# Sums and value tiles copied on chip by DMA, their twelve transposes in float32r in one stretch, and the last two quads' transposes inside the first expert slot

## The chip, the cores and the metric

The kernel runs on one core of a Trainium2 chip. The metric is the device time of one execution in microseconds (us), as a median of runs. TensorE (PE, with its weight loads shown apart as PEld), VectorE (DVE), ScalarE (ACT), GpSimd (POOL) and the queue of SyncE (SP), which issues most of the loads, each work their instructions off in order and wait for one another through semaphores. All the PSUM there is, eight banks, is in use during attention.

## The reference

Attention with capped scores over 8 batches, 12 heads, 448 tokens and 64 dimensions; its output, 3584 tokens of 768 values, goes through a gate that picks one of 8 experts for each token, and through that expert's two matrices.

```python
scores = cap * np.tanh(q @ k.T / 8 / cap)
attn = np.exp(scores); attn /= attn.sum(-1) + 1e-9
x = (attn @ v)                       # 3584 x 768 after the heads are joined
logits = x @ w_gate + modality_bias[modality_id]
e = argmax(logits); gate = softmax(logits)[e]
out = gate * (relu(x @ w1[e]) @ w2[e])   # w1 768 x 1024, w2 1024 x 768
```

## The kernel before

The first 351 us are attention, the rest are expert slots (`run_slots`): blocks of up to 384 gathered tokens of one expert, with `ffn1` (x by w1) and `ffn2` (by w2), each value split into two float32r parts.

Attention is worked by **quads**: a quad is four heads of one batch (two pairs, t = 0 and 1), 24 quads (NQ) in all, three to a batch. Scores stand transposed, keys on the partitions. Six steps of a quad are a pair's 128 keys (t, i), and a seventh (`shared`) takes the last 64 keys of both pairs. Each step makes a score tile `sc` (two PSUM banks, pool `ps_s`, two buffers), ScalarE's tanh (`th`) and exp (`pt`, or `sh`), and TensorE's product with the values (`pv`, `pvs`) into `xT`, one PSUM bank per pair, which stays transposed: features by queries.

The order in which the engines get the work is written out by hand. Step i of the main loop has four rounds R0 to R3, and `ORDER` lists for each round what is done and for which quad (an offset to i). `group` is the scores, tanh and exp of the round; R0 has `shared`, each of the others two steps. `pin` keeps the order as written on every engine's queue; what is not pinned (the routing arithmetic of `route`, which the main loop advances by one stage at the end of a round) may be moved by the scheduler.

After its scores, a quad has this to do. `tot1` and `tot2` (DVE) add its probabilities. `xs` (DVE) copies `xT` out of PSUM. `sums` (PE) makes one PSUM tile of gate logits and sums over keys, `gl` (DVE) copies that to SBUF. `lt` (PE) turns it with four float32 transposes into the one-bank PSUM tile `small`; `den` (DVE) reads it there, makes the reciprocals and scales the logits. `tp` (PE) turns each of the two `xs` tiles with four float32 transposes, into the tile `v` (t = 0, shared with `sums`) or `small` (t = 1); `rows` (DVE) scales them and a DMA from POOL writes them to DRAM (`xd`). Before, `lt`, `tp` of t = 0, `den` and `rows` stand in R3 of the next step, `tp` and `rows` of t = 1 in R0 of the one after that.

`fetch` and `fetch_v` load the next quads' tiles through SP. In R3 of the steps in `SPLITS` (12, 14, 15, 17, 18, 20), `split_w` splits a part of the first expert's w1: a cast on ACT behind the round's exps, and a subtraction on DVE that waits for it; both are pinned. At steps 11 and 20, in R0, `early_expert` and `early_full` count tokens with a small matmul `cps` into `small`. After the 24 quads one more step and a round finish the last quads, with the transposes of the first slot's x among them (`MOVES`), and then `ffn1` of the first slot begins; two callbacks run in it, after its blocks f = 1 (the last routing stage) and f = 2 (the plan of all slots, `slots`), which the next gather waits for.

Of the kernel before, what the change touches and what calls it, by code (L numbers as in the profile page):

```python
# [39 lines left out]
F32 = mybir.dt.float32  # L40
# [10 lines left out]
C, CP = 4, 112  # L51
# [28 lines left out]
class Program:  # L80
# [359 lines left out]
    def attention(self, first, rp):  # L440
        tc, nc = self.tc, self.nc
        pe, pin = nc.tensor, self.pin
        with ExitStack() as st:
# [5 lines left out]
            ps_v = st.enter_context(tc.tile_pool(name="ps_v", bufs=1, space=PSUM))  # L449
            quads = [dict(live=i < NQ, kq={}, hl={}, pt={}, tot={}, xT={}, xs={}) for i in range(NQ + 1)]  # L450

# [53 lines left out]
            def group(q, steps):  # L505

                if q >= NQ:
                    return
                ths = []
                made = [scores(q, *step) if step else shared(q) for step in steps]  # L510
                for sc in made:
                    th = pp.tile([128, 2, S], F32, name="th")
                    pin(nc.scalar.activation(th, sc[:, :, :S], AF.Tanh, scale=self.isc))  # L513
                    ths.append(th)
                for step, th in zip(steps, ths):
                    if step:
                        e = quads[q]["pt"][step] = pp.tile([128, 2, S], F32, name="pt", bufs=8)
# [37 lines left out]
            def xs(q, t):  # L555
                x = quads[q]["xs"][t] = self.lp.tile([128, S], F32, name="xT", bufs=4)
                pin(nc.vector.tensor_copy(x, quads[q]["xT"][t][:, :S]))

            def sums(q):
# [11 lines left out]
            def gl(q):  # L571
                quads[q]["gl"] = t = self.lp.tile([128, S], F32, name="gl")
                pin(nc.vector.tensor_copy(t, quads[q]["glog"][:, :S]))

            def lt(q):
                out = self.ps_r.tile([128, 512], F32, name="lt", tag="small")
                for c in range(C):
                    pin(pe.transpose(out[:CP, c * 128 : (c + 1) * 128], quads[q]["gl"][:, c * CP : (c + 1) * CP], self.ident))
                quads[q]["lt"] = out[:CP].rearrange("p (c x) -> p c x", c=C)
# [23 lines left out]
            def tp(q, t):  # L603
                pool, tag = (self.ps_r, "small") if t else (ps_v, "v")
                out = quads[q]["tp"] = pool.tile([128, 512], F32, name="tp", tag=tag)
                for c in range(C):
                    pin(pe.transpose(out[:CP, c * 128 : (c + 1) * 128], quads[q]["xs"][t][:, c * CP : (c + 1) * CP], self.ident))

            def rows(q, t):
                d = quads[q]  # L610
                if t == 0:
                    d["out"] = self.lp.tile([128, C * 256], F32, name="xs", tag="late", bufs=3)[:CP].rearrange("p (c f) -> p c f", c=C)
                pin(nc.vector.tensor_tensor(
                    d["out"][:, :, t * 128 : (t + 1) * 128].rearrange("p c (j d) -> p c j d", j=2),
                    d["tp"][:CP].rearrange("p (c j d) -> p c j d", c=C, j=2),
                    d["rec"][:, :, t].unsqueeze(3).to_broadcast([CP, C, 2, D]),
                    op=ALU.mult,
                ))
                if t:
# [19 lines left out]
            PICK, KNOWN = 3, 6  # L639
            SPLITS = (12, 14, 15, 17, 18, 20)  # L640
            MOVES = {(NQ, 1): (0, 1), (NQ, 2): (2, 3), (NQ, 3): (4, 5)}
            self.warm(self.ps_r, 4)
# [8 lines left out]
            fetch_v(1)  # L651
            for i in range(NQ + 2):
                for r in (1, 0, 2, 3) if i == 0 else range(4 if i <= NQ else 1):
# [4 lines left out]
                    for op, n, *how in ORDER[r]:  # L658
# [13 lines left out]
                    if (i, r) == (1, 1):  # L672
                        self.empty_map()
                    if (i, r) == (PICK * NH + 2, 0):
# [3 lines left out]
                    if (i, r) == (KNOWN * NH + 2, 0):  # L678
# [8 lines left out]
                    if (i, r) == (NQ - 1, 3):  # L687
                        self.make_x()
                    for k in MOVES.get((i, r), ()):
                        self.transpose(k, ps_s, "sc")  # L690
            self.raws = [self.load_raw(e, self.w2, k, DM) for k in range(self.nstage)]
            way = routing[0]
            next(way)
            return early, way

# [12 lines left out]
    def moe_pools2(self, st):  # L708
        pool = lambda name, bufs, **kw: st.enter_context(self.tc.tile_pool(name=name, bufs=bufs, **kw))
        wp = pool("wp2", 1)  # L710
        self.w2s = [[wp.tile([128, DM], F32R, name=f"b{h}{k}") for h in "hl"] for k in range(FC)]
        self.h = [wp.tile([128, FC, W], F32R, name=f"h{h}") for h in "hl"]
        self.ps_h, self.ps_t, self.ps_y = (
            pool("ps_h", 3, space=PSUM), pool("ps_t", 2, space=PSUM), pool("ps_y", 2, space=PSUM)
        )
# [59 lines left out]

    def transpose(self, k, pool, tag, busy=False, n=TW):
        nc = self.nc
        pt = pool.tile([128, 512], F32, name="ptr", tag=tag)
        w = n * 128
        for t in range(n):  # L780
            move = nc.tensor.transpose(
                pt.bitcast(F32R)[:, t * 128 : (t + 1) * 128], self.xg[:, t, k * 128 : (k + 1) * 128], self.identr
            )
            if t == 0:
                self.pin(move)
        hi, lo = self.x[k][:, 0, :w], self.x[k][:, 1, :w]
        if busy:
            self.pin(nc.vector.tensor_copy(hi, pt[:, :w]))
        else:
            nc.scalar.copy(hi, pt[:, :w])  # L790
        nc.vector.tensor_tensor(lo, pt[:, :w], hi, op=ALU.subtract)  # L791

# [60 lines left out]

    def run_slot(self, cur, n, ahead=None, raws=(), between=()):

# [4 lines left out]
        moves, at = [], {}  # L860
        if n == TW:
            self.load_w2(cur[0], raws, range(len(raws) or FC))
        if raws:
            between = (*between, (between[-1][0], lambda: self.load_w2(cur[0], raws, range(len(raws), FC))))
        nxt = ahead() if ahead and not between else None
# [3 lines left out]
        if n < TW:  # L869
            self.load_w2(cur[0], raws)  # L870
        if nxt and nxt[2]:
            self.load_w1(nxt[0])
            moves = [lambda k=k: self.transpose(k, self.ps_t, "ptr", n=nxt[2]) for k in range(KC)]
        elif nxt:
# [7 lines left out]
            }  # L882
        self.ffn2(cur[1], n, between=moves, wait=2 if raws else 0, at=at)
        return nxt
# [89 lines left out]
    def run_slots(self, cur, order):  # L974
# [17 lines left out]
        for i in range(FIXED + 1):  # L992
            if i == FIXED:
                which = nc.values_load(self.plani[0:1, 2:3], min_val=0, max_val=len(ENDS))
            cur = self.run_slot(cur, TW, lambda: ahead(i), *((self.raws, order) if i == 0 else ()))
        self.finish(which, len(ENDS) - 1, cur, ahead)
# [107 lines left out]
    def tail(self, fresh=False):  # L1104
# [4 lines left out]
        with ExitStack() as st:  # L1109
# [4 lines left out]
            with tc.For_i(begin, total, 1) as s:  # L1114
# [9 lines left out]
                for k in range(KC):  # L1124
                    self.transpose(k, self.ps_t, "ptr")
                self.ffn1(TW)
                self.ffn2(mt, TW)

    def build(self):
        tc, nc = self.tc, self.nc  # L1130
        with ExitStack() as st:
# [4 lines left out]
            with ExitStack() as sa:  # L1136
# [6 lines left out]
                with tc.If(big == 0) as branch:  # L1143
                    with ExitStack() as sb:
# [3 lines left out]
                        rt = sb.enter_context(tc.tile_pool(name="rt", bufs=1))  # L1148
                        early, way = self.attention(first, rt)
                        self.moe_pools2(sb)  # L1150
# [78 lines left out]
```

## Time and profile before

| what | us |
|---|---|
| median of 3 runs | 866.61 |
| lowest and highest | 862.97, 867.07 |
| the profiled execution, its own time | 863.48 |
| its span, first to last instruction | 861.9 |

The profile is of one execution. A row of a timeline has the start in us from the span's beginning, the length in us, the engine, the line, and how many equal instructions are merged; a bracket behind it is idle time of the engine just ahead, with what ended it. PE's instructions overlap, so what a piece costs is the distance from its start to the start of the next piece, not its length.

### The profile page before, as it was taken

Reading aid. Unit: us, or ns where it says so; the run is one execution under the profiler, and the core shown is the slowest. Engines: PE = TensorE matmul, PEld = TensorE weight load, DVE = VectorE, ACT = ScalarE, POOL = GpSimd, SP = SyncE. Lnnn points to the kernel's source line nnn. Section 1 sums busy time; section 2 is a strip of 40 time slices with the busy share of each in tenths; the row PEclk is TensorE's granted clock in tenths of the full one; section 3 lists DMA queues with packets and bytes.
Section 4 is the critical chain, followed back from the end, with each engine's and each line's share of the span. In section 5 each row is a group of like instructions: output and inputs, shape, how many; then the busy total and the mean of one; then the engine's idle time right before and its main releaser. Section 6 shows DMA issues by size and latency. Waiting matters only on the chain. (4 is left out here: it accounts for less than half of the span.)

```text
span 861.9 us, 14828 instructions
## 1 busy us (share of the span) xinstructions
PE 843.7 (98%) x5507; PEld 648.3 (75%) x5507; DVE 528.3 (61%) x1017; ACT 529.3 (61%) x685; POOL 136.1 (16%) x157
## 2 busy tenths in 40 slices
PE   8999999999999999999999999999999999999995
PEld 3444444444444444699999999999999999998884
DVE  6789888989898888874443443444334443428640
ACT  6999999999999899534443443444334444325621
POOL 2002020202020222143102020020301102012101
PEclk9999999999999999999999999999999999999999
DMA  7243435273646351456745255473534745237753
GB/s 252 92 146 89 169 90 169 46 261 89 217 89 217 89 182 41 120 186 201 244 140 190 102 160 215 141 253 106 162 146 159 245 141 185 91 129 228 247 196 125
DMA packets 44024, 136.85 MB, mean 159 GB/s; under 512 B 8470, under 2 KB 8862, under 8 KB 43936
## 3 DMA queue, kind: packets, MB, share of 16 engines
q1 hardware_dynamic: 34544, 102.63, 36.7%
q0 software_dynamic: 9248, 33.11, 11.7%
q8 instruction: 47, 0.77, 0.4%
q14 instruction: 41, 0.34, 0.2%
q10 hardware_dynamic: 144, 0.00, 0.0%
HBM read 113.91 MB, written 22.40 MB: 158 GB/s over the span
## 5 line engine op out<-in xcount | busy, mean ns | idle before, releaser
L513 ACT ACTIVATE th<-sc,isc 128x896 f32<-128x896 f32 x168 | 161.2, 1004 | 22.8 <-PE sc L502 15.4
L812 PE MATMUL ph<-x,al 128*128 128x384 f32 (+1 forms) x480 | 156.1, 325 | 0.0
L839 PE MATMUL py<-bh,hh 128*128 128x384 f32 x448 | 153.5, 343 | 1.6 <-ACT hh L818 1.6
L839 PE MATMUL py<-bh,hl 128*128 128x384 f32 x448 | 150.2, 335 | 0.0
L839 PE MATMUL py<-bl,hh 128*128 128x384 f32 x448 | 149.7, 335 | 0.0
L520 ACT ACTIVATE pt<-th,cabs 128x896 f32<-128x896 f32 x144 | 142.1, 1041 | 0.0
L808 PE MATMUL ph<-x,ah 128*128 128x384 f32 x384 | 129.3, 337 | 0.0
L809 PE MATMUL ph<-x,ah 128*128 128x384 f32 x384 | 129.0, 336 | 0.0
L528 PE MATMUL xT<-pt,va 128*64 128x448 f32 x576 | 125.0, 555 | 0.0
L762 DVE TENSOR_TENSOR bl<-raw,bh 128x768 fp32r<-128x768 f32 x80 | 73.5, 954 | 44.6 <-ACT bh L761 41.6
L844 ACT ACTIVATE ot<-py,mt 128x384 f32<-128x384 f32 x56 | 32.6, 582 | 106.6 <-PE py L839 61.9
L761 ACT CAST bh<-raw 128x768 fp32r<-128x768 f32 x80 | 63.5, 839 | 49.5 <-DMA raw<-in_w_dram 45.3
L818 ACT ACTIVATE hh<-ph 128x384 fp32r<-128x384 f32 x64 | 30.6, 490 | 99.4 <-PE ph L812 96.0
L812 PEld LDWEIGHTS ph<-x,al 128*128 128x128 f32 x480 | 90.2, 188 | 0.0
L849 POOL DMA_INDIRECT out_dram<-ot,mt x28 | 31.4, 1122 | 369.1 <-ACT ot L844 339.8
L839 PEld LDWEIGHTS py<-bh,hh 128*128 128x128 f32 x448 | 84.1, 188 | 3.2 <-ACT hh L818 1.9
L819 DVE SCALAR_TENSOR_TENSOR hl<-ph,hh 128x384 fp32r<-128x384 f32 x64 | 34.7, 554 | 83.4 <-ACT hh L818 83.4
L762 DVE TENSOR_TENSOR al<-raw,ah 128x1024 fp32r<-128x1024 f32 x60 | 71.2, 1222 | 22.9 <-ACT ah L761 22.5
L791 DVE TENSOR_TENSOR x<-ptr,x 128x384 fp32r<-128x384 f32 (+1 forms) x60 | 31.2, 540 | 87.8 <-ACT x L790 87.8
L839 PEld LDWEIGHTS py<-bl,hh 128*128 128x128 f32 x448 | 84.2, 188 | 0.0
L839 PEld LDWEIGHTS py<-bh,hl 128*128 128x128 f32 x448 | 84.1, 188 | 0.0
L528 PEld LDWEIGHTS xT<-pt,va 128*64 128x64 f32 x576 | 35.2, 137 | 63.0 <-issue 43.2
(199 smaller groups left out, 1374.1 us busy)
## 6 DMA issues: line engine op xcount, KB each, us to landing
raw<-in_w_dram SPq DMA_DIRECT2D x66, 512.0 KB, 4.8
raw<-in_w_dram SPq DMA_DIRECT2D x86, 384.0 KB, 5.1
kq<-in_kq_dram SPq DMA_DIRECT2D x47, 448.0 KB, 6.5
va<-in_v_dram SPq DMA_DIRECT2D x24, 448.0 KB, 4.9
xd<-xs POOLq DMA_DIRECT2D x24, 448.0 KB, 5.1
mapd<-pay,pos POOLq DMA_INDIRECT x32, 4.0
xg<-xd,mt POOLq DMA_INDIRECT x30, 5.7
first<-in_kq_dram SPq DMA_DIRECT2D x2, 224.0 KB, 3.3
```

The costliest lines, as they stand in the source:

```text
L513: pin(nc.scalar.activation(th, sc[:, :, :S], AF.Tanh, scale=self.isc))
L520: pin(nc.scalar.activation(e, th, AF.Exp, scale=self.cabs))
L528: pin(pe.matmul(xT[j * D : (j + 1) * D, :S], va[:, u * D : (u + 1) * D], quads[q]["pt"][t, i][:, j], start=i == 0, stop=t == 1 and i == KU ...
L761: a = self.nc.scalar.copy(hi, raw)
L762: b = self.nc.vector.tensor_tensor(lo, raw, hi, op=ALU.subtract)
L808: nc.tensor.matmul(ph[:, :w], hi[:, fs], self.x[k][:, 0, :w], start=first, stop=False)
L809: nc.tensor.matmul(ph[:, :w], hi[:, fs], self.x[k][:, 1, :w], start=False, stop=False)
L812: nc.tensor.matmul(ph[:, :w], lo[:, fs], self.x[k][:, 0, :w], start=False, stop=last)
L819: nc.vector.scalar_tensor_tensor(hl[:, f, :w], acc, 0.0, hh[:, f, :w], op0=ALU.max, op1=ALU.subtract)
L839: nc.tensor.matmul(py[:, :HALF], self.h[a][:, f, rows], self.w2s[f][c][:, cs], start=i == 0, stop=i == 3 * FC - 1,)
L844: nc.scalar.mul(ot[:, cs], py[:, :HALF], mt[:, t, 1:2])
L849: self.last_out = nc.gpsimd.indirect_dma_start(self.out, bass.IndirectOffsetOnAxis(ap=mt.bitcast(I32)[:, t, 0:1], axis=0), ot, None, bound ...
```

## The change

`xs` and `gl` each gain an SBUF-to-SBUF DMA on SP's queue (`again`), which makes a float32r copy of the tile, 128 by 448, for all quads but the last. `turn` transposes that copy with the float32r identity. `lt` and both `tp` move to R0 two steps later, in one stretch of twelve transposes, behind `pvs`. `lt` writes into a buffer of the score pool instead of `small` (for the last two quads still `small`). `den` and both `rows` stand behind them in R0; `tot1` stays ahead of `den`, `tot2` goes behind `xs`. `split_hi` and `split_lo` of the next quad go to R2 and R3. R2 has one `pv` step where it had two, R3 three. `pt` has six buffers instead of eight. The counts at steps 11 and 20 go from R0 to R1. `split_w` stays where it was, at the end of R3. After the last quad one shorter list (`LAST`) is left; the transposes of quads 22 and 23 and the last routing stages run inside `ffn1`, after its blocks 0, 1 and 2, the plan after block 3. The first slot's w2 is split after blocks 2 and 3, no longer ahead of `ffn1`.

```diff
+            def again(q, what, src, tag, bufs):
+                if q < NQ - 1:
+                    copy = quads[q]["cp"][what] = self.lp.tile([128, S], F32R, name="cp", tag=tag, bufs=bufs)
+                    self.load(copy.bitcast(F32), src)
+            def turn(q, what, src, out):
+                copy = quads[q]["cp"].get(what)
+                for c in range(C):
+                    cs, to = slice(c * CP, (c + 1) * CP), slice(c * 128, (c + 1) * 128)
+                    if copy is None:
+                        pin(pe.transpose(out[:CP, to], src[:, cs], self.ident))
+                    else:
+                        pin(pe.transpose(out.bitcast(F32R)[:CP, to], copy[:, cs], self.identr))
...
             def lt(q):
-                out = self.ps_r.tile([128, 512], F32, name="lt", tag="small")
+                if q < NQ - 2:
+                    out = ps_s.tile([128, 2, 512], F32, name="sc")[:, 0]
+                else:
+                    out = self.ps_r.tile([128, 512], F32, name="lt", tag="small")
+                turn(q, "gl", quads[q]["gl"], out)
...
             ORDER = (
-                ((group, 0, (None,)), (pvs, -1), (tp, -2, 1), (tot1, -1, 1), (tot2, -1, 1), (rows, -2, 1), (xs, -1, 0)),
-                ((group, 0, ((0, 0), (0, 1))), (pv, -1, 1, 1), (pv, -1, 1, 2), (split_hi, 1, 0), (xs, -1, 1), (split_lo, 1, 0)),
                 (
-                    (group, 0, ((0, 2), (1, 0))), (sums, -1), (pv, 0, 0, 0), (pv, 0, 0, 1),
-                    (split_hi, 1, 1), (split_lo, 1, 1), (gl, -1), (tot1, 0, 0),
+                    (group, 0, (None,)), (pvs, -1), (lt, -2), (tp, -2, 0), (tp, -2, 1), (tot1, -1, 1), (den, -2),
+                    (rows, -2, 0), (rows, -2, 1), (xs, -1, 0), (tot2, -1, 1),
+                ),
+                ((group, 0, ((0, 0), (0, 1))), (pv, -1, 1, 1), (pv, -1, 1, 2), (xs, -1, 1)),
+                (
+                    (group, 0, ((0, 2), (1, 0))), (sums, -1), (pv, 0, 0, 0),
+                    (split_hi, 1, 0), (split_lo, 1, 0), (gl, -1), (tot1, 0, 0),
                 ),
                 (
-                    (group, 0, ((1, 1), (1, 2))), (lt, -1), (tp, -1, 0), (pv, 0, 0, 2), (pv, 0, 1, 0),
-                    (tot2, 0, 0), (den, -1), (rows, -1, 0),
+                    (group, 0, ((1, 1), (1, 2))), (pv, 0, 0, 1), (pv, 0, 0, 2), (pv, 0, 1, 0),
+                    (split_hi, 1, 1), (split_lo, 1, 1), (tot2, 0, 0),
                 ),
             )
+            LAST = (
+                ((pvs, -1), (tot1, -1, 1), (xs, -1, 0), (tot2, -1, 1)),
+                ((pv, -1, 1, 1), (pv, -1, 1, 2), (lt, -2), (xs, -1, 1)),
+                ((sums, -1), (gl, -1)),
+                ((den, -2),),
+            )
...
-                        self.run_slots(early, ((1, lambda: next(way, None)), (2, order)))
+                        w2 = lambda at, *ks: (at, lambda: self.load_w2(early[0], self.raws, range(*ks)))
+                        self.run_slots(early, (*late, w2(2, 0, 4), (3, order), w2(3, 4, FC)))
```

`late` holds three callbacks: after block 0, `tp` of quad 22, `lt` of quad 23, `rows` and `den`; after block 1, `tp` and `rows` of quad 23 and two routing stages; after block 2, the last routing stage.

## Rows read from the trace of the kernel before

**Rows 1.** The page: busy time, share and count of PE, and the granted TensorE clock in 40 slices of the span, in tenths.

```profile
PE 843.7 (98%) x5507; PEld 648.3 (75%) x5507; DVE 528.3 (61%) x1017; ACT 529.3 (61%) x685; POOL 136.1 (16%) x157
PEclk9999999999999999999999999999999999999999
```

**Rows 2.** Busy time by stretch, for a stretch of attention. Columns: length, busy time of each engine, granted clock, DMA share, GB/s.

```profile
50.00:150.00 100.00, 100.00 (x744) 48.06 (x740) 85.09 (x174) 93.19 (x102) 14.47 (x17) 1.00 0.42 130
```

**Rows 3.** Who waited for whom over the whole span: total us, times, longest.

```profile
ACT th L513 <- PE sc L502: 15.4, 23, 3.8
...
SPq L92 <- PE xT L528: 238.8, 20, 14.7
```

**Rows 4.** The timeline of PE over one quad without a cast and without routing, from its first score step (R1) to the next quad's.

```profile
122.93 0.47 PE L502 MATMUL sc<-hi 64*128 64x448 f32 x2
...
124.34 1.72 PE L528 MATMUL xT<-pt,va 128*64 128x448 f32 x8
...
127.41 0.56 PE L569 MATMUL glog<-tot,pick 128*32 128x448 f32 x1
...
129.05 1.72 PE L528 MATMUL xT<-pt,va 128*64 128x448 f32 x8
130.71 0.47 PE L502 MATMUL sc<-hi 64*128 64x448 f32 x2
...
132.11 0.65 PE L578 MATMUL lt<-ident,gl 128*112 128x128 f32 x4
132.60 0.60 PE L607 MATMUL tp<-ident,xT 128*112 128x128 f32 x4
133.13 1.72 PE L528 MATMUL xT<-pt,va 128*64 128x448 f32 x8
134.78 0.98 PE L490 MATMUL sc<-kq 64*64 64x448 f32 x8
...
136.45 0.65 PE L607 MATMUL tp<-ident,xT 128*112 128x128 f32 x4
137.03 0.47 PE L502 MATMUL sc<-hi 64*128 64x448 f32 x2
```

**Rows 5.** The timeline of PE around two runs of six float32r transposes (of x): among full-size matmuls of the first slot, and after the last quad among attention's smaller forms.

```profile
398.55 0.64 PE L781 MATMUL ptr<-identr,xg 128*128 128x128 f32 x6
399.03 0.41 PE L839 MATMUL py<-bh,hh 128*128 128x384 f32 x1
...
354.37 0.70 PE L781 MATMUL ptr<-identr,xg 128*128 128x128 f32 x6
355.00 0.56 PE L569 MATMUL glog<-tot,pick 128*32 128x448 f32 x1
```

**Rows 6.** The timeline of PE at the count of step 11.

```profile
164.86 0.65 PE L607 MATMUL tp<-ident,xT 128*112 128x128 f32 x4
166.29 0.17 PE L290 MATMUL cps<-acc,ones 112*128 112x8 bf16 x1 [0.78 <-DVE xs L613]
```

**Rows 7.** The timeline of ACT: the exp of `shared` in quads 12 and 20, eight quads apart, and in quad 14 the tanh pair of R3, and the cast of `split_w` behind the exps.

```profile
180.42 1.04 ACT L520 ACTIVATE sh<-th,cabs 128x896 f32<-128x896 f32 x1
...
295.57 1.04 ACT L520 ACTIVATE sh<-th,cabs 128x896 f32<-128x896 f32 x1
...
218.21 1.91 ACT L513 ACTIVATE th<-sc,isc 128x896 f32<-128x896 f32 x2 [0.42 <-PE sc L502]
...
221.87 1.04 ACT L761 CAST ah<-raw 128x1024 fp32r<-128x1024 f32 x1
```

**Rows 8.** The same R3 of quad 14: PE's first score step, and the timeline of DVE: the first and the last of `den`'s six instructions, `split_w`'s subtraction, `tot1`.

```profile
217.23 0.47 PE L502 MATMUL sc<-hi 64*128 64x448 f32 x2
...
219.34 0.17 DVE L585 COPY rec<-lt 112x16 f32<-112x16 f32 x1 [0.80 <-PE lt L578]
...
220.11 0.36 DVE L594 TENSOR_TENSOR lg<-lt,rec 112x64 f32<-112x64 f32 x2
...
222.93 1.23 DVE L762 TENSOR_TENSOR al<-raw,ah 128x1024 fp32r<-128x1024 f32 x1 [1.87 <-ACT ah L761]
224.08 1.08 DVE L549 TENSOR_TENSOR tot<-pt 128x896 f32<-128x896 f32 x1
```

**Rows 9.** The timeline of DVE in the quad of rows 4: the copy `gl` behind `sums`.

```profile
129.19 0.62 DVE L573 COPY gl<-glog 128x448 f32<-128x448 f32 x1
```

**Rows 10.** The timeline of PE at the end of attention: the last quad's `pvs`, and the first matmul of `ffn1`.

```profile
351.22 0.98 PE L539 MATMUL xT<-sh,va 64*64 64x448 f32 x8
...
360.67 0.44 PE L808 MATMUL ph<-x,ah 128*128 128x384 f32 x1
```

**Rows 11.** DMA issues: count, KB each, median us from issue to landing.

```profile
kq<-in_kq_dram SPq DMA_DIRECT2D x47, 448.0 KB, 6.5
va<-in_v_dram SPq DMA_DIRECT2D x24, 448.0 KB, 4.9
...
xg<-xd,mt POOLq DMA_INDIRECT x30, 5.7
first<-in_kq_dram SPq DMA_DIRECT2D x2, 224.0 KB, 3.3
```

**Rows 12.** The timeline of POOL: the last gather of the second slot's tokens.

```profile
386.28 1.00 POOL L745 DMA_INDIRECT xg<-xd,mt  x1 [0.30 <-PE ph L812]
```

More of the change, by code (lines that the diff above doesn't have):

```diff
@@ L516, in group @@
                     if step:
-                        e = quads[q]["pt"][step] = pp.tile([128, 2, S], F32, name="pt", bufs=8)
+                        e = quads[q]["pt"][step] = pp.tile([128, 2, S], F32, name="pt", bufs=6)
                     else:
@@ L573, in gl @@
                 pin(nc.vector.tensor_copy(t, quads[q]["glog"][:, :S]))
+                again(q, "gl", t, "cg", 1)
             def lt(q):
-                out = self.ps_r.tile([128, 512], F32, name="lt", tag="small")
-                for c in range(C):
-                    pin(pe.transpose(out[:CP, c * 128 : (c + 1) * 128], quads[q]["gl"][:, c * CP : (c + 1) * CP], self.ident))
+                if q < NQ - 2:
[3 more added lines that the diff above has]
+                turn(q, "gl", quads[q]["gl"], out)
                 quads[q]["lt"] = out[:CP].rearrange("p (c x) -> p c x", c=C)
@@ L603, in tp @@
             def tp(q, t):
[L604 to L607, printed above, removed]
+                pool, tag = (self.ps_t, "ptr") if q >= NQ - 2 else (self.ps_r, "small") if t else (ps_v, "v")
+                out = quads[q]["tp"][t] = pool.tile([128, 512], F32, name="tp", tag=tag)
+                turn(q, t, quads[q]["xs"][t], out)
             def rows(q, t):
@@ L688, in attention, with before, last @@
                         self.make_x()
-                    for k in MOVES.get((i, r), ()):
-                        self.transpose(k, ps_s, "sc")
-            self.raws = [self.load_raw(e, self.w2, k, DM) for k in range(self.nstage)]
-            way = routing[0]
-            next(way)
-            return early, way
+                    if (i, r) == (NQ, 1):
+                        moved = [turn_two(0, 1), turn_two(2, 3)]
+                        self.split_x(*moved[0])
+                    if (i, r) == (NQ, 2):
+                        self.split_x(*moved[1])
+                        self.split_x(*turn_two(4, 5))
+            self.raws = [self.load_raw(e, self.w2, k, DM) for k in range(self.nstage)]
+            def before():
+                tp(NQ - 2, 0)
+                tp(NQ - 2, 1)
+                lt(NQ - 1)
+                rows(NQ - 2, 0)
+                rows(NQ - 2, 1)
+                den(NQ - 1)
+            def last():
+                tp(NQ - 1, 0)
+                tp(NQ - 1, 1)
+                rows(NQ - 1, 0)
+                rows(NQ - 1, 1)
+                next(routing[0])
+                next(routing[0])
+            return early, ((0, before), (1, last), (2, lambda: next(routing[0], None)))
     def moe_pools(self, st):
@@ L774, in load_w2, with transpose, turn_x @@
             self.split_w(raw, self.w2s[k], pin=bool(raws))
[L776 to L779, printed above, removed]
+    def transpose(self, k, n=TW):
+        pt = self.ps_t.tile([128, 512], F32, name="ptr")
+        self.turn_x(k, pt, n)
+        self.split_x((k,), (pt,), n)
+    def turn_x(self, k, pt, n=TW):
         for t in range(n):
-            move = nc.tensor.transpose(
+            move = self.nc.tensor.transpose(
                 pt.bitcast(F32R)[:, t * 128 : (t + 1) * 128], self.xg[:, t, k * 128 : (k + 1) * 128], self.identr
@@ L785, in transpose, with split_x @@
                 self.pin(move)
[L786 to L791, printed above, removed]
+    def split_x(self, ks, pts, n=TW):
+        w = n * 128
+        for k, pt in zip(ks, pts):
+            self.nc.scalar.copy(self.x[k][:, 0, :w], pt[:, :w])
+        for k, pt in zip(ks, pts):
+            self.nc.vector.tensor_tensor(self.x[k][:, 1, :w], pt[:, :w], self.x[k][:, 0, :w], op=ALU.subtract)
     def ffn1(self, n, between=()):
@@ L852, in ffn2, with run_slot @@
             )
-    def run_slot(self, cur, n, ahead=None, raws=(), between=()):
+    def run_slot(self, cur, n, ahead=None, between=()):
         moves, at = [], {}
[L861 to L864, printed above, removed]
+        if n == TW and not between:
+            self.load_w2(cur[0])
         nxt = ahead() if ahead and not between else None
@@ L869, in run_slot @@
         if n < TW:
-            self.load_w2(cur[0], raws)
+            self.load_w2(cur[0])
         if nxt and nxt[2]:
             self.load_w1(nxt[0])
-            moves = [lambda k=k: self.transpose(k, self.ps_t, "ptr", n=nxt[2]) for k in range(KC)]
+            moves = [lambda k=k: self.transpose(k, n=nxt[2]) for k in range(KC)]
         elif nxt:
@@ L1148, in build @@
                         rt = sb.enter_context(tc.tile_pool(name="rt", bufs=1))
-                        early, way = self.attention(first, rt)
+                        early, late = self.attention(first, rt)
                         self.moe_pools2(sb)
```

32 lines of the change are left out of this document (19 added, 13 removed).

## The prediction, made before the changed kernel was run

> **What bounds the kernel.** I read the page first, then attention's busy times by stretch, the list of waits, and PE's timeline over one quad. PE is busy 98% of the span, at a granted clock of nine tenths or more in every slice (1.00 in the stretch of attention, the 2.4 GHz level) [rows 1, 2]. Busy is not yet bound, since PE's instructions overlap. What settles it is PE's timeline of a quad: the pieces follow one another with no gap from 122.93 to 137.03, so a quad takes 14.10 us and that is the sum of PE's pieces [rows 4]. ACT, busy 93.2 of 100 us, has 13.1 us of work in a quad, and what it waits for is PE's scores [rows 2, 3]. DVE is busy 85.1 of 100 us, 12.0 in a quad [rows 2]. So a microsecond taken from PE is worth one until ACT's floor of some 13.2, and DVE has two spare microseconds to be late in, as long as nothing on PE hangs on the late instruction.
>
> **Part 1, the transposes of a steady quad.** Before, the piece in R3 (eight transposes) costs 132.11 to 133.13, 1.02 us, and the one in R0 (four) 136.45 to 137.03, 0.58 [rows 4]. Both end with a change of the tile shape in the array. Without the R3 piece the score step goes straight to `pv`, at no more than it paid: the same step costs 1.41 where `pv` follows (122.93 to 124.34) and 1.40 where `lt` does [rows 4]. So 1.60 goes out. The new stretch is bounded by the two runs of six float32r transposes: 0.48 among matmuls of like shape, 80 ns each, and 0.63 with a change of shape behind it, hence 0.15 for the change and the start [rows 5]. Twelve at 80 ns and one change make 1.11 us. The trace does not show 112 columns in float32r; the bounds are 75 ns (80 less the share of columns that are missing) and the fp32 rate, 132.11 to 132.60 for four, 122 ns [rows 4]. I take 80, by the nearest form. A quad gains 0.49, 22 quads (i = 2 to 23) gain **10.8**; a period of 13.6 is still over ACT's floor. Quad 1, which loses its R3 piece too, sits near that floor; I count nothing there.
>
> [...]
>
> **Part 2, the two counts.** At step 11 the count matmul stands behind a transpose of R0 and waits for `rows` to free `small`: 1.43 from 164.86 to 166.29, where the piece costs 0.58 [rows 4, 6]. In R1 `small` is read by then. The matmul keeps its own start and change of shape, so 0.7 for each of two: **1.4**.
>
> **Part 3, what the casts cost before.** From quad 12 to quad 20 eight quads take 115.15 us, 2.3 over eight times 14.10 [rows 4, 7]. ACT's casts push PE there, and the small routing matmuls are in it too; 1.7 I put to the casts. In the changed order it is the next part that carries them, so this comes off: **1.7**.
>
> **Part 4, a new wait on PE.** The score pool has two buffers. With `lt` in it, R0 takes both (`shared`, `lt`), and the second score step of R1 must wait until `den`, DVE's last reader of `lt`, is done. Behind that step wait all of PE's queue and then ACT's tanh. In a plain quad it just fits. From the start of `shared` (0): `shared` and `pvs` 1.67, transposes 1.11, first step half of 1.41, so the second step wants its buffer at 3.49 [rows 4]. `lt`'s four end near 2.2, and `den` takes 219.34 to 220.47, 1.13 [rows 8]: done at 3.3. Ahead of `den` stands `tot1`, 1.0, which is ready near 0.3.
>
> In the quad after a cast it does not fit. DVE's `al` waits for ACT's cast, which stands behind R3's exps, and `tot1` and `den` stand behind `al`. In quad 14 `tot1` started 6.85 after R3's first score (217.23 to 224.08), DVE having waited 1.87 for the cast [rows 8]; before, `den` and `rows` were done by then. In the new order `shared` comes 3.8 after R3's first score (1.41, and three `pv` steps, 2.4 by the 1.66 that two cost) [rows 4]. So `tot1` starts at 3.05, `den` ends at 3.05 + 1.0 + 1.13 = 5.2, and PE stands 1.7. Six casts make 10.2. In the step after a routing quad, the routing stages have made DVE late, and `den` with it. Bounds are 0 and 1.2 (all the arithmetic that a routing quad adds in its last round, and no slack); I take 0.3, since the slack of a plain quad is about as long, in seven quads: 2.1. Together **+12.3**, bounds 0 and 6 times 2.0 plus 7 times 1.2, 20.
>
> **Part 5, the copies.** Three SP issues of 224 KB a quad. SP stood idle before, ahead of its work (238.8 us of waits for `pv` to free `va`) [rows 3]; now the copies hold it in step, so `fetch` runs a quad later, still more than a quad ahead of use. The two `xs` copies have over 8 us. `gl`'s is the tight one: it ends 2.4 after `sums` begins (127.41 to 129.81) [rows 4, 9], and `lt` stands `sums` 1.64, `pv` 0.9, scores 1.41, `pv` 2.4, `shared` and `pvs` 1.67 behind that beginning, 8.0; 5.6 us are left. The trace has no copy on chip. The nearest rows: the same size from DRAM, 3.3 us, and the tiles that share the queue, 4.9 and 6.5 [rows 11]. By the row of like size, nothing. Buffers: `pt` at six still frees each a round or more ahead.
>
> The Trainium skill, "DMA: Bandwidth & Descriptors", § Latency and other measured facts, gives some 2 us as a DMA's fixed cost. By it the copy would land sooner than any of these rows, and the sum stays.
>
> **Part 6, the end of attention.** Before, `pvs` of the last quad to `ffn1` takes 351.22 to 360.67, 9.45 [rows 10]. After: `pvs` 0.9, `pv` 1.65, `lt` and twelve x transposes 1.4, `sums` 1.64, six more 0.63, then `ffn1`; in its first two blocks eight transposes at 80 and twelve at 120 ns. That is 6.2 + 2.1 = 8.3: **1.1** less. The plan of the slots comes a block (3.1 us), two sets of transposes and some w2 splits later on DVE, some 6 us against `ffn1`'s start. The last gather issued at 386.28 landed 5.7 later, near 393, and its first reader stands at 398.55 [rows 5, 11, 12], 1.4 us later in the new order by its own added transposes. I take it as hidden; if not, 1 to 2 us.
>
> **Sum.** −10.8 − 1.4 − 1.7 + 12.3 − 1.1 = −2.7, against the profiled execution's 863.48: 860.8. The median of the runs shown, 866.61, lies 3.1 above that execution, and the lowest run at its level; I put my number half way up, **862.3**. A measurement of this kernel tells 0.5%, some 4.3 us, from no change.
>
> **Rivals.**
>
> First, *the new wait is not there*: `den` is read in time, since the scheduler finds another place or the cast is done sooner. For it: DVE has 2 us to spare in a quad. Against: `pin`, and the order in rows 8. Parts 1, 2 and 6 then count in full, but ACT (13.2 plus a cast of 1.04 [rows 7]) keeps about half of what the casts cost, and DVE some of the routing: −8 to −9, 855, and 856.5 on my level.
>
> Second, slower: *`gl`'s copy lands late*. From 5.6 us on, every further microsecond is one on PE, since `lt` heads the stretch, and `den` and the score step follow. At the 6.5 of `kq` [rows 11] that is 0.9 in 22 quads, 20 us: 882. For it: other tiles on the same queue; against: it is half their size and stands ahead of the next one.
>
> Third, *float32r gains no rate*: 120 ns as now. The stretch is 1.59, the 10.8 go; the later start of the second step gives back some 0.45 in each of the six waits and the 2.1 of routing, so about +3.5: 867, no change that can be told.
>
> Fourth, *the second slot's rows are late*: forecast and 2 us, 864.
>
> **Chances.** Forecast 0.48 (its own range 857 to 867, from 75 to 84 ns and waits of 8 to 16), no wait 0.20, late copy 0.13, no rate 0.09, late rows 0.10. Faster by over 0.5%: the no-wait case and four tenths of the forecast, 0.38. Slower: the late copy and a few of the others, 0.17. The range takes in the no-wait case and the partly late copy: 854 to 871.
>
> **What the new profile would show.** Quads without cast or routing at 13.6 us; twelve transposes in 1.0 to 1.1; PE standing 1.7 ahead of the second score step in six quads, released by DVE's `den`; DVE waiting about 2 us for the cast ahead of it. Landing of the copies under 5 us and no wait of `lt` for a DMA. `ffn1` about 3 us nearer to the last `pvs`. Wrong would be: waits of PE for a DMA in R0, or no wait at `den`.

## The result and the profile after

The changed kernel takes **876.91 us** (median of 4 runs, 874.65 to 878.68), the kernel before 865.81 beside it (862.97 to 867.07): 1.0143 times as long, 95% interval 1.0123 to 1.0164. It is slower by 1.4%, and the forecast of 862.3 us, with its range up to 871, was too low.

The profiled execution is of 877.24 us, with a span of 875.6 against 861.9. The instants of both timelines divide those 13.7 us:

| stretch | before, us | after, us | difference |
|---|---|---|---|
| start to the exp of `shared` in quad 12 | 180.42 | 175.97 | −4.45 |
| from there to the last `pvs` | 170.80 | 186.56 | +15.76 |
| last `pvs` to the first `ffn1` | 9.45 | 6.67 | −2.78 |
| first `ffn1` to the first `ffn2` | 25.38 | 27.25 | +1.87 |
| first `ffn2` to the second slot's `ffn1` | 26.63 | 29.63 | +3.00 |
| from there to the end | 449.21 | 449.49 | +0.28 |

For half of the attention the change wins about what was asked of it, though 1.64 us of that come before quad 2 begins, where the prediction counted nothing; then the second half gives back more than three times as much, and the first slot 3 us. The first scores of quad 2, before and after:

```profile
35.65 0.98 PE L490 MATMUL sc<-kq 64*64 64x448 f32 x8
```

```profile
34.01 0.98 PE L490 MATMUL sc<-kq 64*64 64x448 f32 x8
```

The page's rows of PE and of its clock, against [rows 1], and the two waits on PE that [rows 3] does not have:

```profile
PE 838.3 (96%) x5507; PEld 643.4 (73%) x5507; DVE 528.0 (60%) x1017; ACT 529.4 (60%) x685; POOL 133.3 (15%) x157
PEclk9999999989999999999999999999999999999999
```

```profile
PE sc L502 <- DVE lg L613: 9.5, 11, 1.6
PE sc L573 <- DMA cp<-gl: 8.1, 4, 4.3
```

PE is busy 5.4 us less and ends 13.7 later. Two things on it now wait: the second score step (`sc`) for `den`, whose last instruction writes `lg`, and the transposes of the sums for the copy of `gl`. The ninth digit of the clock is an 8.

A quad with neither wait (a plain quad), on PE's timeline (start, duration, line, operation; `tp` holds both value tiles):

```profile
47.71 0.98 PE L490 MATMUL sc<-kq 64*64 64x448 f32 x8
48.52 0.93 PE L539 MATMUL xT<-sh,va 64*64 64x448 f32 x8
49.38 0.50 PE L573 MATMUL sc<-identr,cp 128*112 128x128 f32 x4
49.72 0.77 PE L573 MATMUL tp<-identr,cp 128*112 128x128 f32 x8
50.42 0.47 PE L502 MATMUL sc<-hi 64*128 64x448 f32 x2
...
51.99 1.72 PE L528 MATMUL xT<-pt,va 128*64 128x448 f32 x8
...
61.41 0.98 PE L490 MATMUL sc<-kq 64*64 64x448 f32 x8
```

The period is 13.70 us against 14.10 [rows 4]. The quad whose copy came latest, and the busy times of PE and the other engines around it (columns as in [rows 2]):

```profile
179.88 0.67 PE L573 MATMUL sc<-identr,cp 128*112 128x128 f32 x4 [4.33 <-DMA cp<-gl]
```

```profile
176.00:179.00 3.00, 0.00 (x0) 0.00 (x0) 0.00 (x0) 1.01 (x1) 0.46 (x2) 1.00 1.04 246
179.00:182.00 3.00, 2.12 (x16) 1.99 (x18) 1.31 (x7) 0.00 (x0) 0.38 (x1) 0.51 0.81 286
182.00:185.00 3.00, 3.00 (x16) 1.77 (x14) 2.43 (x4) 1.91 (x3) 0.71 (x1) 0.50 0.20 56
185.00:188.00 3.00, 3.00 (x22) 1.37 (x18) 1.30 (x3) 2.44 (x4) 0.00 (x0) 0.85 0.61 180
```

PE stands still for 4.33 us; while it stands, the granted clock falls to 0.5, the 1.2 GHz level, and stays there for about 6 us after work has begun again (to 185.9). So the quad takes 20.52 us: 13.70, 4.39 of wait (counted from when the transposes could have started), and 2.43 that neither has. The same happens in two more places of this execution, behind a 1.60 us wait for `den` (quad 13: 17.29 = 13.70 + 1.76 + 1.83) and a 1.90 us wait for the copy (quad 18: 16.90 = 13.70 + 1.97 + 1.23). Before, no microsecond of the attention from 20 us on was at the lower level.

What made the copy late is in the DMA rows of the stretch 160 to 176 us (issues: count, KB each, median us to landing; GB/s in 40 slices of 0.4 us), SP's issue of the copy, and two stretches in the columns of [rows 2]:

```profile
GB/s 206 367 397 403 394 305 63 9 0 0 0 2 0 0 1 132 390 54 2 152 376 72 0 54 9 27 54 18 81 99 45 54 27 27 18 343 427 373 424 370
...
kq<-in_kq_dram SPq DMA_DIRECT2D x2, 448.0 KB, 9.4
...
cp<-gl SPq DMA_DIRECT2D x1, 224.0 KB, 9.0
mapd<-pay,pos POOLq DMA_INDIRECT x4, 6.4
```

```profile
170.77 0.48 SPq L92 DMA_DIRECT2D cp<-gl  x1
```

```profile
168.80:174.00 5.20, 5.20 (x36) 2.20 (x36) 5.13 (x7) 5.19 (x7) 0.00 (x0) 1.00 0.68 39
174.00:176.00 2.00, 1.55 (x16) 0.33 (x12) 1.31 (x2) 1.78 (x3) 0.00 (x0) 1.00 1.09 388
```

The copy needed 9.0 us, and had 4.7: it was issued at 170.77, and the transposes could have started at 175.49. From 168.8 to 174 us next to nothing moves, 39 GB/s, although loads and the copy are queued; the DMA engines do not stand still (their busy share is 0.68), so the few packets of that time take long. In front of it stand the four indirect writes of the token map that `route` issues on POOL from 163.11 to 168.1. The other copies behind such writes are slow too: 5.5, 6.3, 5.0 and 4.9 us in quads 6, 9, 15 and 21. Over this kernel's whole span the median of `gl`'s copy is 3.1 us, about what Part 5 assumed.

### The profile page after: what moved, and what is told of

Read it like the earlier page. It is cut to its first block, busy times and chain, and to the rows that moved or that the text cites. A ratio compares the mean times of both kernels' runs of the same rounds, so it can differ in the third digit from the quotient of the medians.

```text
span 875.6 us, 14993 instructions
## 1 busy us (share of the span) xinstructions
PE 838.3 (96%) x5507; PEld 643.4 (73%) x5507; DVE 528.0 (60%) x1017; ACT 529.4 (60%) x685; POOL 133.3 (15%) x157
## 5 line engine op out<-in xcount | busy, mean ns | idle before, releaser
L846 DVE TENSOR_TENSOR x<-ptr,x 128x384 fp32r<-128x384 f32 (+1 forms) x54 | 28.0, 538 | 84.1 <-ACT x L844 84.1
```

## The experiments

Fourteen kernels, all built from the changed one. Times are medians, and a ratio is to the kernel before, timed on the same chip beside them.

**Float32 sums.** The copy of `gl` goes, the copies of the values stay:

```
 def gl(q):
     ...
-    again(q, "gl", t, "cg", 1)
```

> The copy of the sums (`gl`) is dropped and `lt` turns them in float32 from the tile itself; the copies of the values and everything else stay. Theory A, that most of the loss is `lt` waiting for that copy (8.5 us of waits in quads 6, 9, 12, 18 and 22, and 3 to 4 us of matmuls at the lower clock behind them): these waits vanish, four transposes in each of 22 quads start 109 ns apart and not 77 (+2.8 us), so 866 to 869 us. Theory B, that most of it is the second score step waiting for `den` behind the weight split (1.76 us in five quads, 0.41 in six): those waits stay and quad 18 gets its own, the time goes to 878 to 880 us.

Measured: 871.3 us, ratio 1.0064 (1.0045 to 1.0084). Between the two theories. No transpose waits for a copy any more, but the wait for `den` is all there, and now one in quad 18 too, which the late copy had hidden:

```profile
PE sc L502 <- DVE lg L612: 10.1, 9, 1.6
```

In the profiled execution, the longest of the five (875.61 us), five of its six long waits (1.6 us each) were followed by 3 to 4 us at the lower level, and those quads take 17.2 to 17.7 us, where 13.85 is plain.

**Late splits.** The other suspect alone: the weight splits move behind `den`.

```
-if r == 3 and i in SPLITS:
-    k = SPLITS.index(i)
+if r == 1 and i - 1 in SPLITS:
+    k = SPLITS.index(i - 1)
```

> The six weight splits of the early expert move from round 3 of their step to round 1 of the next, behind `den`; the copies stay. Theory B: the 1.76 us waits in quads 13, 15, 16, 19 and 21 vanish (8.8 us, and up to 1.5 us of lower clock), 866 to 869 us. Theory A: the late copies stay and show in quad 18 in full, 873 to 877 us. The six waits of 0.41 us behind the routing stay by either. The weights are loaded half a step later, which nothing waits for before quad 22.

Measured: 876.54 us, 1.0128 (1.0106 to 1.0150), the number of theory A. The wait for `den` fell as B said, and the wait for the copy grew:

```profile
PE sc L573 <- DMA cp<-gl: 13.3, 6, 6.1
PE sc L502 <- DVE lg L613: 2.2, 6, 0.5
```

The growth is not the edit's work alone. In quads 12 and 15 the copies had as long as before (4.7 and 5.6 us), but took 10.7 and 6.9 us, against 9.0 and 5.0 in the profile of the changed kernel; in another profile of that kernel (the run “Writes later, first try”, below) they took 10.9 and 6.8, and the waits for copies came to 11.1 us. Neither of the two causes can be sized by taking it away alone.

**No map writes.** The four writes are left out for the first seven samples. The expert slots then move fewer rows, so the total can't be compared, and only the attention is read.

```
-for c in range(C):
+for c in range(C if tok is not None or b == B - 1 else 0):
     put = nc.gpsimd.indirect_dma_start(self.mapd, ...)
```

> The four indirect writes of the token map are left out for the first seven of the eight samples, so most tokens get no row in the output and what follows the attention moves fewer rows; only the attention (up to the last `pvs`) is to be read. Theory A1, that the copies are late because DMA packets of every queue are slow for some 5 us behind those writes: the waits for the copy in quads 6, 9, 12 and 18 vanish (7.3 us and 3 to 4 us of lower clock), the last `pvs` starts at 351 to 353 us and not at 362.5. Theory A2, that the copies are late through the load that they, the kq, value and weight loads put on the engines themselves: the waits stay within 2 us, last `pvs` at 360 to 363 us.

The wait for the copy is gone but for one of 0.2 us:

```profile
PE sc L502 <- DVE lg L613: 10.8, 10, 1.6
PE sc L573 <- DMA cp<-gl: 0.2, 1, 0.2
```

So A1 names the cause rightly: with these writes out, the same copies in the same queue land in time; in the stretch from 158 to 174 us `kq` takes 4.5 us and `gl` 4.9, where it was 9.4 and 9.0. The last `pvs` was at 358.5, not at 351 to 353: five of the six `den` waits were followed by the lower clock, as in the run with float32 sums. Why the writes slow other packets is not shown.

**Writes later, first try.** Two more pauses in `route`, just ahead of the writes.

> Two more pauses in the routing of all samples but the last: the four indirect writes of the token map are issued two rounds later, after the copy of the sums and not ahead of it. Nothing is left out. Theory A1 (the writes slow what is issued behind them): the waits for the copy in quads 6, 9, 12 and 18 vanish, 10 to 11 us, so 865 to 868 us, unless the slow packets now fall on something that is waited for. Theory A2 (load of the copies themselves): 875 to 878 us.

Measured: 881.13 us, 1.019 (1.017 to 1.021). This tested nothing: on POOL the writes stand where they stood (163.09 to 168.1), as nothing lies between on that engine and the positions that they wait for were not moved. No engine's order differs from the changed kernel's, so it is that kernel once more, and shows that its time lies between 874.65 and 882.23 us from one sitting to another. The granted clock differs too: 0.984 or 0.985 over each of these four executions, 0.984 to 0.994 over the four of the result.

**Both at once.** Float32 sums and late splits.

> The sums are turned in float32 (no copy of them) and the weight splits come behind `den`: both waits go at once. Theory C, that the loss is these two waits and the 3.5 to 4 us at the lower granted clock that each long one leaves behind, so that taking away one lets the other show: no wait above 0.5 us on the transposes or the second score step, no stretch at the lower clock between 20 and 360 us, plain quads of 13.85 us, last `pvs` at 346 to 349 us (351.65 before) and 859 to 863 us in all. Rival D, that the order itself loses it (the splits moved, the casts, the two steps' distance of `lt`), whatever these two waits do: last `pvs` above 354 us and 867 us or more.

Measured: **861.13 us** (860.26 to 862.97), ratio 0.9969 (0.9954 to 0.9984), so faster than both kernels. Last `pvs` at 346.7, plain quads 13.85, no lower clock between 20 and 360 us, and of the two waits only this is left on PE:

```profile
PE sc L502 <- DVE lg L612: 2.1, 7, 0.5
```

Theory C holds, D falls. Together the two edits are worth 15.8 us by the medians; alone they were worth 5.6 and 0.4. Beside the two single edits the changed kernel itself ran at 881.13 (the run before this one); by that they are worth 9.8 and 4.6, and the two together 20.0, still more than the sum.

**First w2 splits earlier.** `w2(2, 0, 4)` becomes `w2(1, 0, 4)`.

> Of the changed kernel only the place of the first four w2 splits moves, from behind the third to behind the second column block of the first `ffn1`; the copies and the splits of w1 stay. If the first slot's 3.0 us are lost because the `raw` buffers come free late: from the start of the first `ffn2` to the second slot's `ffn1` 27 to 28 us and not 29.63, with `py`'s waits for `ot` (1.9 us) gone, and 1.5 to 3 us less in all than the changed kernel (874 to 877 us). If they are lost elsewhere (the plan, the gather): the same 29.6 us, or `hh` and `hl` late by what the splits put ahead of them.

Measured: 877.91 us, 1.0145 (1.0102 to 1.0189). The second slot's `ffn1` comes 29.2 us after `ffn2`, and `py`'s waits for `ot` are 2.0 us: hardly moved, and not the 27 to 28 us expected; one block earlier is not enough.

**No copies, float32 throughout.** `again` does nothing.

> All copies are left out and every transpose runs in float32 from the tile itself, in the new order: the change without its first part. If float32r is worth 32 ns a transpose (109 against 77 ns from start to start): plain quads of 14.08 to 14.1 us, as before, +5.6 us against the run with float32 sums alone, 876 to 880 us with the waits for `den` still there. If the copies themselves slow the rest (the queue of loads, the packets): less than that, 870 to 873 us.

Measured: 867.77 us, 1.0052 (1.0033 to 1.0070), below either expectation. Plain quads take 13.98 us. And although `den` is waited for in six quads, no stretch is at the lower level:

```profile
194.38 0.47 PE L502 MATMUL sc<-hi 64*128 64x448 f32 x2 [1.51 <-DVE lg L613]
```

```profile
192.00:195.00 3.00, 1.49 (x13) 1.01 (x12) 2.86 (x9) 1.92 (x2) 0.00 (x0) 1.00 0.00 0
195.00:198.00 3.00, 3.00 (x24) 1.53 (x20) 2.97 (x6) 2.65 (x3) 0.67 (x1) 1.00 0.14 17
```

PE stands 1.29 to 1.58 us there, not 1.60, since slower transposes fill part of the time until `den`. These quads take 15.5 to 16.0 us; in the changed kernel those of its quads that kept the clock take 15.5 to 15.7 (16.0 in one). Where `den` decides, float32r buys nothing.

**Four edits.** Float32 sums, late splits, `w2(1, 0, 4)`, and `den` ahead of `tot1` in R0.

> Four edits on the changed kernel: float32 sums without a copy, weight splits behind `den`, the first four w2 splits behind the second column block, and `den` ahead of the first addition of the row sums (`tot1`) in round 0, so that the second score step no longer waits 0.36 to 0.47 us after the routing. By theory C and the size of these waits: 2 to 3 us below the run with the first two edits for w2 and 2 to 3 us for `den`, 854 to 859 us; by D 862 us or more.

Measured: 865.34 us, 1.0006 (0.9989 to 1.0024) and not the 854 to 859 us that the sizes of the waits gave. The waits for `den` are gone, but a quad after a routing one takes 15.0 us where it took 14.05, and one after a split 15.7, not 14.8. What is late in its place was not followed; `tot1`, which now stands behind `den`, is the first suspect. The second slot's `ffn1` came 1.1 us sooner after the first one's.

**Writes later, in earnest.** Late splits, all copies, and three pauses ahead of the rank matmul, for every sample but the sixth and eighth.

> The weight splits come behind `den`, all three copies stay, and the rank, map positions and four indirect writes of the token map of every sample but the sixth and the eighth come three rounds later, behind the issue of the next copy of the sums. Nothing is left out. Theory A1, that only what is issued behind those writes is slow: the waits of `lt` in quads 6 to 18 are below 0.5 us, plain quads stay at 13.70 us, and the time is 2 to 3 us below the run with float32 sums and late splits (861.1), 857 to 861 us; quad 22, which has no such writes ahead of its copy in this run either, may still lose 2 to 4 us. Theory A2, that the load of the copies is enough: 870 us or more.

Measured: 864.32 us, 0.9996 (0.9973 to 1.0019); 12 us below the run with late splits alone. In quad 12 the writes are now issued from 173.78 to 178.6, behind the copy, and of its wait of 6.1 us 0.77 is left. Up to 200 us the waits for copies are 1.0 us in place of 6.4. Past 200 us it is still 6.9, in other quads, with one of 3.43 us:

```profile
PE sc L576 <- DMA cp<-gl: 7.8, 6, 3.4
PE sc L505 <- DVE lg L616: 0.5, 1, 0.5
```

Ahead of that one's copy SP issues a `kq` tile and a weight tile of 512 KB. A1 holds for what it was read from, but the lateness moves with the writes; with weight loads about, no place for them was found that hurts nobody.

**The w2 splits spread, and the plan sooner.** On top of the two good edits:

```
-(*late, w2(2, 0, 4), (3, order), w2(3, 4, FC))
+(w2(0, 0, 2), *late[:2], w2(1, 2, 4), late[2], (3, order), w2(3, 4, FC))
```

and in the second run `(2, order)`.

> On top of float32 sums and late splits (861.1 us): the first two w2 splits stand behind the first column block of the first `ffn1`, ahead of the work of the attention's end, the next two behind the second block. If the slot loses its time because `raw` comes free late (first w2 cast 11.9 us after `ffn1` begins, 2.6 us in the kernel before), the loads and the w1 casts behind them come 6 to 8 us earlier, `py` no longer waits 1.8 us for `ot`, and 1.5 to 3 us go: 858 to 860 us. If the splits on VectorE only push the attention's end back, the first `ffn1` grows by 1 to 2 us and nothing is won: 861 to 862 us.

> As the run with the w2 splits spread, and the plan of the slots stands behind the third column block of the first `ffn1` and not behind the fourth, so that the gather of the second slot starts some 3 us earlier. If the gather (0.2 us of waits by the x transposes) is the next thing behind `ot`: 0.2 to 1 us less than the run with the spread splits, 857.5 to 860 us; if VectorE's plan chain delays `hl`, up to 1 us more.

Measured: 862.97 us, 0.9984 (0.9970 to 0.9999), and 865.52 us, 1.0008 (0.9997 to 1.0019). Nothing is won on the 861.13 without these edits (0.9969, 0.9954 to 0.9984): the first can't be told from it, the second is slower. The wait for `ot` went, and another came. The first of the two, waits and clock:

```profile
PE ptr L834 <- DMA xg<-xd,mt: 2.3, 2, 1.4
```

```profile
394.00:397.00 3.00, 0.67 (x6) 0.44 (x4) 0.32 (x1) 0.58 (x1) 1.65 (x3) 0.96 1.02 371
397.00:400.00 3.00, 3.00 (x13) 3.00 (x13) 1.02 (x2) 0.86 (x2) 1.07 (x1) 0.50 0.79 274
```

The x transposes wait for the gather, while the DMA engines are full (share 1.02), and the clock falls. That it is the loads started earlier by the freed `raw` buffers which hold up the gather fits, but was not tested. In the second run this wait is 4.5 us, although the plan is earlier.

**No copies, late splits.** What float32r is worth with nothing in its way.

> No copies, every transpose in float32, and the weight splits behind `den`: the new order without its first part and without the wait. Against the run with float32r values and late splits (861.1 us) it shows what float32r is worth where nothing else is in its way: 13.98 against 13.85 us a quad, +2.9 us, 863 to 865 us. Against the run without copies and with the early splits (867.8 us) it shows the price of the wait in float32, where no stretch at the lower clock followed it: 3 to 5 us less. If the copies cost something that the quads do not show, it comes out at 861 us or below.

Measured: 863.81 us, 0.9993 (0.9980 to 1.0007), as expected. Plain quads 13.98 against 13.85, and 2.7 us in the medians. Against the run without copies and with early splits it is 4.0 us less, the price of the six waits where no lower clock follows them.

**The sums turned twice.** Float32 sums with the early splits, and the four transposes of the sums done again into the same place. All other work is unchanged.

> The run with float32 sums and early splits, whose sums are turned twice into the same place: four more float32 transposes, some 0.44 us, in each of 22 quads. Theory L, that the length of the idle decides: the idle of the second score step falls from 1.6 to some 1.2 us, no stretch at the lower clock follows, the six quads with it go to 15.5 to 15.6 us; 5 x 1.8 us come back and 16 x 0.44 us are paid, 868 to 871 us. Theory F, that float32r values decide: the stretches at the lower clock stay, and the time goes up by 7 us to 878 us.

In the profiled execution all is as theory L says. PE waits 1.16 to 1.44 us in the six quads, the clock stays at 1.00 (192 to 201 us, the quad that fell in the run with float32 sums):

```profile
197.27 0.47 PE L502 MATMUL sc<-hi 64*128 64x448 f32 x2 [1.20 <-DVE lg L614]
```

```profile
195.00:198.00 3.00, 1.80 (x16) 1.14 (x14) 2.86 (x9) 1.82 (x2) 0.00 (x0) 1.00 0.01 3
198.00:201.00 3.00, 3.00 (x22) 1.53 (x20) 2.97 (x7) 2.76 (x3) 0.67 (x1) 1.00 0.01 3
```

and those quads take 15.6 to 16.0 us, 1.5 to 1.7 less than the five that lost the clock took without the added work. The time does not follow: 874.84 us, 1.0110 (1.0085 to 1.0134), above the 1.0064 of the run with single transposes. The 16 other quads pay 0.43 us each, 6.9, and the run it is compared with has executions 4 to 6 us shorter than its profiled one. The granted clock of each execution tells why: 0.988 in that profiled one and 0.991 or 0.992 in its four others, 0.996 or 0.997 in all four here. A clock higher by 0.005 over 871 us is some 9 us less at the lower level, an estimate of two to three such stretches and 4 to 5 us, less than the 6.9 paid. So with the added transposes, and values still in float32r, the clock is kept in every execution. The changed kernel loses it in more than its profiled execution: 0.990 there, 0.984, 0.987 and 0.994 in the others, where the kernel before has 0.992 to 0.998 in all its executions beside these runs.

**The two good edits with late writes.** Float32 sums, late splits, and the routing moved as above.

> Float32 sums without a copy, weight splits behind `den`, and the rank, positions and map writes of every sample but the sixth and eighth three rounds later. If the waits behind the routing (`den`, and the value transposes for the rank's PSUM tile) come from where the routing's VectorE work stands: quads after routing go from 14.05 to 13.85 us and from 14.85 to 14.5 us, 1.5 to 2.5 us in all, 858.5 to 860 us. If the moved writes slow the loads that the score steps wait for, or VectorE is late elsewhere: 861 to 864 us.

Measured: 866.06 us, 1.0007 (0.9992 to 1.0021) on a chip where the kernel before takes 866.22. The waits behind the routing fell (`den` 0.5 us in all), but a new one is larger:

```profile
PE sc L505 <- ACT th L516: 6.9, 16, 0.8
```

Seven quads now take 14.9 to 15.5 us. The routing's work on VectorE sits in R2 then, and ACT, which feeds the score steps, is late there; which of its inputs is behind was not followed up.

## Why the prediction was wrong

**Part 1 was right, and a fifth too large.** Forecast a stretch of 1.11 us and a period of 13.6; measured 1.04 (49.38 to 50.42) and 13.70, so 0.40 a quad in place of 0.49, 8.8 us over 22 quads if nothing else decided. What the shorter stretch wins and the period does not show is lost right behind it: the score step there takes 1.57 (50.42 to 51.99) in place of 1.41. The prediction's lower bound of 75 ns a transpose does not come out of its own reason, since 80 less an eighth is 70; the sum went by 80. The float32 runs split this: 0.12 for one stretch instead of two (14.10 to 13.98), 0.13 for the values in float32r (13.85), 0.15 for the sums (13.70). The third rival, no rate from float32r, falls. The Trainium skill, "TensorE: Matmul & The Clock Gate", Part 4, gives about 275 ns for a transpose, most of it access latency. For float32 the rows agree with the figure, 273 to 285 ns mean; in float32r the mean is 245 to 252 ns here, and the quad is shorter.

**Parts 2 and 3.** The steps with a count went from 15.07 to 14.20 and from 15.29 to 14.20 us; less the 0.40 of Part 1 that is 1.2 against 1.4. The casts' own cost can't be told apart from what follows.

**Part 4 was right in mechanism and size.** PE stands 1.60 us (1.76 late) in five quads and is 0.41 late in six, 11.3 us against 12.3; the sixth of the long waits was hidden behind a late copy. The first rival falls. What the part left out is what a long stop does to TensorE's clock.

**Part 5 is the step that failed.** It set the slack of `gl`'s copy, 5.6 us, against a median landing time, 3.3, and its second rival against another median, 6.5 in all 22 quads. The median was right (3.1), and so was the slack of a plain quad; what counts is the tail, and in quad 12, where the arithmetic of the count makes VectorE late with `gl`, the slack was 4.7. Five copies came late, by 0.12, 0.84, 4.39, 1.97 and 1.16 us, 8.5 together, and four of the five in the quads behind `route`'s writes. The trace of before had the same holes. Behind the writes that POOL issued from 249.98 to 255.4 the DMA engines were busy for 4 us (share 0.99) and moved 33 GB/s:

```profile
256.00:260.00 4.00, 4.00 (x36) 1.61 (x32) 3.96 (x6) 4.00 (x6) 0.00 (x0) 1.00 0.99 33
```

Nothing on PE hung on a DMA of that moment then, and I read only medians and waits. The run without the writes shows the cause; the runs with float32 sums show that the waits go with the copy. The Trainium skill, "DMA: Bandwidth & Descriptors", § Issuing engines are not separate DMA queues, says that DMAs from different issuers share the same 16 engines. The trace agrees: POOL's four writes hold up SP's copy, 9.0 us, against 4.9 without them.

**Not in the sum: the clock.** Three stops in the profiled execution were followed by the 1.2 GHz level; by the quads' periods that is 2.43 + 1.83 + 1.23, 5.5 us. The clock is full before [rows 1, 2], and I took that for a property of the kernel, where it was one of a PE queue without holes. The prediction set this term at nothing without a reason.

**Part 6 was right up to `ffn1` and wrong behind it.** −2.78 + 1.87 = −0.9, forecast −1.1. But what was taken "as hidden; if not, 1 to 2 us" cost 3.0, and not by the gather, for which no transpose of x waits: `py` waits 1.9 us for `ot`, which on ACT stands behind casts of the next `w1` that wait for `raw`:

```profile
381.14 3.02 ACT L813 CAST bh<-raw 128x768 fp32r<-128x768 f32 x4
...
410.81 1.05 ACT L813 CAST ah<-raw 128x1024 fp32r<-128x1024 f32 x1 [2.72 <-DMA raw<-in_w_dram]
411.76 0.58 ACT L899 ACTIVATE ot<-py,mt 128x384 f32<-128x384 f32 x1
```

The first w2 cast comes 11.9 us after `ffn1` begins (381.14 against 369.20), before 2.6 (363.23 against [rows 10]), so the buffers come free 9 us later against the work. I followed the plan past `ffn1`, not the loads that the splits release. With the splits earlier the gather came late instead, so for this slot only the wait is shown, not a cure; the other 1.1 us were not traced.

Put into the sum, the measured terms give −2.7 + 2.0 (Part 1) − 1.0 (Part 4) + 8.5 + 5.5 + 3.0 = 15.3, against 13.7 in the spans. The 1.6 too much is about what the two quads of the start give, 1.64, which the prediction set at nothing; the cause of that was not followed.

## What to carry to other kernels

Before a transfer goes onto the path, set its slack against its late landings and ask what other queues issue just ahead of it: a median that fits says little about the quads that decide. Where one of two waits is taken away and the time stays, take away both before judging either; here 0.4 and 5.6 us alone were 15.8 together (4.6, 9.8 and 20.0 by the other sitting). And price a stop of a busy TensorE by its wait and by the clock behind it: the version that won gives up the fastest transposes (0.15 us a quad) to have no stop of more than half a microsecond there.

## What was not expected of the hardware

Four indirect writes, 112 rows of 8 bytes each, were followed by 5 us in which the DMA engines, at a busy share of 0.68, moved 39 GB/s: a copy that landed in 3.1 us in the median took 9.0.

A PE wait of 1.6 us was enough to be followed by 3 to 4 us at half the clock, in 14 of 25 such waits of the profiled executions of five runs (the changed kernel and its second profile, float32 sums, without the map writes, the earlier w2 splits), while twelve waits of 1.16 to 1.58 us in two others were not, none of them; adding 0.43 us of useless transposes ahead of such a wait made five of those quads 1.5 to 1.7 us shorter in the profiled executions. All nine waits of over 2 us in the attention of the profiled executions were followed by it. But the length of one wait is not all that decides: one of 1.95 us kept the clock (quad 16 of the run with writes later, in earnest), two of 0.63 and 1.03 us within 4 us lost it (quad 21 of the changed kernel's second profile). What else does is open.
